# Narrow head-by-head loads and 64x64 attention tiles for nine of twenty-four chunks of a retention + MoE kernel

One core of one Trainium2 chip. The metric is the device time of one execution in microseconds, the slowest (here the only) core's; lower is better.

## The reference, cut to what matters

Linear attention with a decaying state for 4 batches, 8 heads, 768 tokens, head width 64; its output, 3072 tokens by 512, goes through a feed-forward block.

```python
for t in range(S):                        # attention, per batch and head
    state = gamma * state + outer(k[t], v[t])
    y[t] = scale * q[t] @ state
h = x @ w_in                              # x: 3072 x 512, w_in: 512 x 2048
s = np.sin(alpha * h)
out = (h + s * s / (alpha + 1e-09)) @ w_out
```

## The kernel before

The tokens are cut into 24 chunks of 128. Within a chunk attention is computed with masked scores; between chunks a 64x64 state per head is carried. Four first chunks of the batches come first, then the rest batch by batch. I call the index into `order` the *place* of a chunk, from 0: places 14 to 18 are chunks 1 to 5 of batch 2, places 19 to 23 those of batch 3.

```python
order = [b * NCH for b in range(B)]
order += [b * NCH + c for b in range(B) for c in range(1, NCH)]

def load_chunk(j, names="qkv"):           # 3 DMAs of 128 tokens x 8 heads x 64, float32 -> bfloat16
    ...
    nc.gpsimd.dma_start(out=t, in_=chunk_of(src, j))

def scale_v(j, eng):                      # v times its decay
    eng.tensor_mul(raw["v", j], raw["v", j], kg[:, j % NCH, :, None].to_broadcast([128, H, D]))

def turn(j):                              # q and k transposed by DMA, issued by SyncE
    nc.sync.dma_start_transpose(out=st["qkT", j], in_=raw["qk", j].rearrange("p i h d -> p (i h d)"))

def stage_A(j):                           # scores of a pair of heads: 64 rows x 128 columns
    for p in range(NP):
        for e in range(2):
            r = slice(64 * e, 64 * e + 64)
            nc.tensor.matmul(pa[:, e, p, :], qkT[r, NP + p, :], qkT[r, p, :], ...)
    nc.vector.tensor_mul(aT, pa, m)       # causal mask

def stage_M(j):                           # state times q, then v times scores; 128 rows x 64 columns
    ...
    nc.tensor.matmul(py[r, p, :], s_bd[c % 2][:, p, r], qkT[:, p, :], ...)
    ...
    nc.tensor.matmul(py[64 * e:64 * e + 64, p, :], vs[:, 2 * p + e, :], aT[:, e, p, :], ...)
    ps = stage_S(j) if c < NCH - 1 else None      # k times v into the state

# GpSimd's list: one in-order queue for loads and scalings
for n in range(11, NJ + 2):
    scale_v(P[n - 2], nc.gpsimd)
    if n < NJ:
        load_chunk(P[n])
    ...
```

The feed-forward block runs all the time: slots of four 512-column `ph` (w_in) and four `po` (w_out) multiplications. At fixed slots an attention burst is put between them: scores of place n, then output and state of place n-1.

## Time and profile before

| | before |
|---|---|
| time, median of the first 3 runs | 217.23 us (216.76 to 217.30) |
| span of the profiled run | 216.0 us |
| TensorE busy | 202.8 us, 94% |
| VectorE, ScalarE, GpSimd busy | 59%, 75%, 42% |
| GpSimd's loads (q0) | 13.37 MB, 88% of 16 engines' span |

"Busy" counts what an engine works on. q0 is the DMA queue of the loads that GpSimd issues; at 88% on average over the whole run it was full while it was used, for it is empty after 124 us. A *piece* of a load is the 64 numbers of one token of one head. The prediction shows the page's slices, the burst and GpSimd's list. A row of a timeline is: start and duration in us, engine, source line, operation, names, shapes, count, and in brackets the idle time before it and what ended it.

### The profile page before, as it was taken

The numbers are of one execution on the slowest core, as the hardware profiler recorded it, in microseconds if no ns is written. First come the engines' busy times: TensorE is split into PE (matmuls) and PEld (weight loads), VectorE is DVE, ScalarE is ACT, GpSimd is POOL, SyncE is SP. The second block draws the span as 40 slices with busy tenths as digits, with TensorE's granted clock in tenths as the row PEclk, the third lists the DMA queues.
The fourth block names the chain that finished last, engine by engine and source line by source line (L and its number), as shares of the span: only waits on it lengthen the run. The fifth ranks groups of instructions, "written<-read, shape, count | busy, mean of one in ns | idle before, by whom it ended". The sixth has DMA issues, their size and how long they took to land.

```text
span 216.0 us, 4277 instructions
## 1 busy us (share of the span) xinstructions
PE 202.8 (94%) x1658; PEld 108.5 (50%) x1685; DVE 127.9 (59%) x213; ACT 162.6 (75%) x311; POOL 90.0 (42%) x105
## 2 busy tenths in 40 slices
PE   7888898899989999999999999999999999999994
PEld 2444553457664555454554544554544544555554
DVE  5786759774896777765565565664644545333311
ACT  7778796468879988897787787787778877666630
POOL 8975332999395977786987200000000000000000
PEclk9999999999999999999999999999999999999999
DMA  9999999999999999999999942141011001111112
GB/s 130 154 189 189 206 207 167 143 116 214 185 138 194 123 151 173 131 177 146 174 146 144 126 100 71 26 102 50 2 49 52 15 33 49 52 49 49 52 49 97
DMA packets 100852, 24.93 MB, mean 115 GB/s; under 512 B 93392, under 2 KB 97888, under 8 KB 100832
## 3 DMA queue, kind: packets, MB, share of 16 engines
q0 software_dynamic: 77024, 13.37, 88.1%
q1 hardware_dynamic: 23808, 11.28, 26.3%
q8 instruction: 13, 0.21, 0.4%
q14 instruction: 7, 0.06, 0.1%
HBM read 27.27 MB, written 6.29 MB: 155 GB/s over the span
## 4 chain that ended last, share of the span: by engine, by line
PE 73%; DMA 13%; POOL 4%; DVE 4%; issue 2%; ACT 2%; POOLq 0%; DVEq 0%
PE po L304 32%; PE ph L279 30%; DMA qkr<-in_k_dram 8%; DMA w_in<-in_moe_w_in_dram 4%; PE py L247 3%; PE pa L213 2%; POOL qkr L83 2%; PE py L251 2%; PE poh L327 2%; DVE gT L294 2%; DVE aT L217 1%; POOL vr L83 1%; PE ps L227 1%; DVE xT L258 1%; ACT s L282 1%
## 5 line engine op out<-in xcount | busy, mean ns | idle before, releaser
L294 DVE SCALAR_TENSOR_TENSOR gT<-s,rec_alpha,ph 128x512 bf16<-128x512 f32 (+3 forms) x120 | 74.2, 638 | 71.5 <-ACT s L287 71.2
L279 PE MATMUL ph<-xT,w_in 128*128 128x512 bf16 (+3 forms) x477 | 97.7, 336 | 1.0 <-DMA w_in<-in_moe_w_in_dram 0.4
L282 ACT ACTIVATE s<-ph,alpha_sb 128x512 f32<-128x512 f32 (+3 forms) x120 | 69.6, 601 | 32.9 <-PE ph L279 32.4
L304 PE MATMUL po<-w_out,gT 128*128 128x512 bf16 x345 | 90.4, 379 | 3.3 <-issue 2.4
L279 PEld LDWEIGHTS <-w_in 128*128 128x128 bf16 x480 | 45.4, 98 | 42.1 <-issue 1.1
L287 ACT ACTIVATE s<-s 128x512 f32<-128x512 f32 (+1 forms) x94 | 58.4, 621 | 2.6
L304 PEld LDWEIGHTS <-gT 128*128 128x128 bf16 x368 | 33.9, 98 | 36.7 <-issue 0.6
L112 POOL TENSOR_TENSOR vr<-vr,kg 128x512 bf16<-128x512 bf16 x21 | 21.9, 1054 | 18.3 <-DMA vr<-in_v_dram 18.1
L217 DVE TENSOR_TENSOR aT<-pa,mask 128x1024 bf16<-128x1024 f32 x20 | 24.4, 1222 | 0.2 <-PE pa L213 0.2
L83 POOL DMA_DIRECT2D vr<-in_v_dram x24 | 21.8, 908 | 3.2 <-DMA w_in<-in_moe_w_in_dram 1.7
L83 POOL DMA_DIRECT2D qkr<-in_q_dram x23 | 21.3, 927 | 3.9 <-DMA w_out<-in_moe_w_out_dram 2.0
L83 POOL DMA_DIRECT2D qkr<-in_k_dram x23 | 20.5, 893 | 4.9 <-DMA w_out<-in_moe_w_out_dram 4.6
L234 ACT CAST s_bd<-ps 64x256 bf16<-64x256 f32 x40 | 14.4, 360 | 2.6 <-PE ps L227 2.1
L316 ACT COPY o_sb<-po 128x512 f32<-128x512 f32 x23 | 13.1, 576 | 3.9 <-PE po L304 3.7
L258 DVE TENSOR_TENSOR xT<-py,qg 128x512 bf16<-128x512 f32 x20 | 13.7, 684 | 1.3 <-PE py L251 1.3
L213 PE MATMUL pa<-qkT 64*128 64x128 bf16 x192 | 9.5, 219 | 1.2 <-DMA qkT<-qkr 0.6
L213 PEld LDWEIGHTS <-qkT 64*128 64x128 bf16 x192 | 5.4, 94 | 10.2 <-issue 6.7
L345 PE MATMUL spare<-warm 128*128 128x512 bf16 x27 | 9.0, 455 | 1.4 <-DVE warm L131 1.2
L251 PE MATMUL py<-aT,vr 128*64 128x128 bf16 x192 | 9.5, 220 | 0.4 <-DVE aT L217 0.4
L247 PE MATMUL py<-qkT,s_bd 128*64 128x128 bf16 x160 | 8.3, 225 | 0.0
L251 PEld LDWEIGHTS <-vr 128*64 128x64 bf16 x192 | 6.8, 110 | 1.3 <-issue 1.0
L247 PEld LDWEIGHTS <-s_bd 128*64 128x64 bf16 x160 | 5.1, 109 | 3.2 <-ACT s_bd L234 0.8
(61 smaller groups left out, 74.3 us busy)
## 6 DMA issues: line engine op xcount, KB each, us to landing
out_dram<-o_sb SPq DMA_DIRECT2D x23, 256.0 KB, 2.2
vr<-in_v_dram POOLq DMA_DIRECT2D x24, 128.0 KB, 6.3
qkr<-in_q_dram POOLq DMA_DIRECT2D x23, 128.0 KB, 5.6
qkr<-in_k_dram POOLq DMA_DIRECT2D x23, 128.0 KB, 5.9
w_in<-in_moe_w_in_dram POOLq DMA_DIRECT2D x4, 512.0 KB, 11.1
w_out<-in_moe_w_out_dram POOLq DMA_DIRECT2D x4, 512.0 KB, 15.0
qkT<-qkr SPq DMA_TRANSPOSE x17, 6.4
q<-in_q_dram SPq DMA_DIRECT2D x1, 256.0 KB, 3.3
```

Of the source, the lines that this page charges most:

```text
L83: nc.gpsimd.dma_start(out=t, in_=chunk_of(src, j))
L112: eng.tensor_mul(raw["v", j], raw["v", j], kg[:, j % NCH, :, None].to_broadcast([128, H, D]))
L213: nc.tensor.matmul(pa[:, e, p, :], qkT[r, NP + p, :], qkT[r, p, :], start=(p == 0), stop=True, skip_group_check=True)
L217: nc.vector.tensor_mul(aT.rearrange("p e n t -> p (e n) t"), pa.rearrange("p e n t -> p (e n) t"), m)
L247: nc.tensor.matmul(py[r, p, :], s_bd[c % 2][:, p, r], qkT[:, p, :], start=(p == 0), stop=True, skip_group_check=True)
L251: nc.tensor.matmul(py[64 * e:64 * e + 64, p, :], vs[:, 2 * p + e, :], aT[:, e, p, :], start=(c == 0 and p == 0), stop=True, skip_group_che ...
L258: nc.vector.tensor_mul(x, py, qg[:, c])
L279: nc.tensor.matmul(self.ph[:, m, :], w_in[:, i, f * 128:(f + 1) * 128], xT[g][:, i, self.lo:self.hi], start=(m == 0 and i == 0), stop=(i = ...
L282: nc.scalar.activation(out=self.s[:, m, :], in_=self.ph[:, m, :], func=ACTF.Sin, scale=alpha_sb[:, f:f + 1])
L287: nc.scalar.activation(out=self.s, in_=self.s, func=ACTF.Square)
L294: nc.vector.scalar_tensor_tensor(gT[self.g][:, f, self.lo:self.hi], self.s[:, m, :], rec_alpha[:, f:f + 1], self.ph[:, m, :], op0=ALU.mult ...
L304: nc.tensor.matmul(po[g, ts], gT[g][:, f, ts * C:(ts + 1) * C], w_out[:, f, :], start=(f == 0), stop=(f == FF - 1))
```

## The change

Nine chunks (places 15 to 18 and 19 to 23) become *wide*: heads 0 to 3 lie in partitions 0 to 63 and heads 4 to 7 in 64 to 127, tokens in halves of 64. Scores, mix and state then run in four 64x64 tiles of the array, and the masked quarter of the scores is skipped. Loads go head by head, for four or five chunks at once. The state is added up in SBUF by VectorE. In a wide burst, `inter` is state times q, `scores` is k times q of the next chunk, and `mix` is v times scores, followed by k times v into the state; `mix` needs the scaled v.

```diff
+    def load_seq(bt, names="qkv"):
+        ...
+            for h in range(H):
+                r = slice(64 * (h // NP), 64 * (h // NP) + 64)
+                o = tv[r, :, h % NP, :] if name == "v" else tqk[r, :, "qk".index(name), h % NP, :]
+                nc.gpsimd.dma_start(out=o, in_=src[bt, h, cs[0] * C:, :].rearrange("(f i) d -> i f d", i=64))
...
+    tiles4 = [(b, e) for b in range(2) for e in range(2)]
+    def scores(j):
+        for m in range(2):
+            for b, e in tiles4:
+                nc.tensor.matmul(pa[half(b), e, 192 * m:192 * m + 128]..., qkT[half(e), 2 + m, half(b)], ...)
+            for b, e in tiles4:
+                nc.tensor.matmul(pa[half(b), e, 192 * m + 128:192 * m + 192], qkT[half(e), 6 + m, half(b)], ...)
...
+    def burst(old, new, first=None):
+        inter(old)
+        return {**(scores(new) if new is not None else {}), **mix(old, first)}
...
-    for n in range(11, NJ + 2):
-        scale_v(P[n - 2], nc.gpsimd)
-        if n < NJ:
-            load_chunk(P[n])
-        ...
+    load_chunk(P[11])
+    scale_v(P[9], nc.gpsimd)
+    load_chunk(P[12])
+    scale_v(P[10], nc.gpsimd)
+    load_chunk(P[13])
+    scale_v(P[11], nc.gpsimd)
+    load_chunk(P[14])
+    scale_v(P[12], nc.gpsimd)
+    load_seq(2, "qk")
+    scale_v(P[13], nc.gpsimd)
+    scale_v(e2, nc.gpsimd)
+    scale_v(P[14], nc.gpsimd)
+    load_seq(2, "v")
+    scale_v(e3, nc.gpsimd)
+    load_seq(3, "qk")
+    for n in range(15, 19):
+        scale_v(P[n], nc.gpsimd)
+    load_seq(3, "v")
```

In the list the scaling of place 15 stands *behind* all q and k loads of batch 3.

More of the change, by code (lines that the diff above doesn't have):

```diff
@@ L77, in load_chunk @@
             if name == "v":
-                t = big.tile([128, H, D], BF16, name="vr", tag="vr", bufs=NJ)
+                t = big.tile([128, H, D], BF16, name="vr", tag="vr", bufs=NJ - 9)
             else:
                 if ("qk", j) not in raw:
-                    raw["qk", j] = big.tile([128, 2, H, D], BF16, name="qkr", tag="qkr", bufs=NJ)
+                    raw["qk", j] = big.tile([128, 2, H, D], BF16, name="qkr", tag="qkr", bufs=NJ - 10)
                 t = raw["qk", j][:, "qk".index(name)]
@@ L84, in load_chunk, with wide @@
             raw[name, j] = t
+    def wide(j):
+        return j >= 2 * NCH + 2 and j != 3 * NCH
+    def load_seq(bt, names="qkv"):
+        cs = [c for c in range(NCH) if wide(bt * NCH + c)]
+        nh = 2 * len(cs)
+        if "q" in names:
+            raw["seq", bt] = (big.tile([128, nh, 2, NP, D], BF16, name=f"qk_seq{bt}"),
+                              big.tile([128, nh, NP, D], BF16, name=f"v_seq{bt}"))
+        tqk, tv = raw["seq", bt]
+        for name, src in (("q", q), ("k", k), ("v", v)):
+            if name not in names:
+                continue
+            for h in range(H):
+                r = slice(64 * (h // NP), 64 * (h // NP) + 64)
+                o = tv[r, :, h % NP, :] if name == "v" else tqk[r, :, "qk".index(name), h % NP, :]
+                nc.gpsimd.dma_start(out=o, in_=src[bt, h, cs[0] * C:, :].rearrange("(f i) d -> i f d", i=64))
+        for i, c in enumerate(cs):
+            j, f = bt * NCH + c, slice(2 * i, 2 * i + 2)
+            raw["qk", j], raw["k", j], raw["v", j] = tqk[:, f], tqk[:, f, 1], tv[:, f]
     WP = 4
@@ L98 @@
     for name, src in (("q", q), ("k", k)):
-        near[name] = big.tile([128, H, D], F32, name=f"{name}0")
+        near[name] = work.tile([128, d_model], F32, name="o_sb", tag="o_sb", bufs=3).rearrange("i (h d) -> i h d", h=H)
         nc.sync.dma_start(out=near[name], in_=chunk_of(src, 0))
@@ L111, in scale_v @@
     def scale_v(j, eng):
-        eng.tensor_mul(raw["v", j], raw["v", j], kg[:, j % NCH, :, None].to_broadcast([128, H, D]))
+        t, by = raw["v", j], kg
+        if wide(j):
+            t, by = t.rearrange("i f p d -> i (f p) d"), kgq
+        eng.tensor_mul(t, t, by[:, j % NCH, :, None].to_broadcast([128, H, D]))
     load_chunk(0, "v")
@@ L157, with later_tables, later_mask @@
                          lg[:, None, :].to_broadcast([128, NCH, H]))
+    kgq = consts.tile([128, NCH, H], F32, name="kgq")
+    expoq = consts.tile([128, NCH, H], F32, name="expoq")
+    tok = consts.tile([128, NCH, 2], F32, name="tok")
+    lgq = consts.tile([128, NP], F32, name="lgq")
+    maskq = consts.tile([128, 192], BF16, name="maskq")
+    def later_tables():
+        for b in range(2):
+            r = slice(64 * b, 64 * b + 64)
+            for f in range(2):
+                nc.vector.tensor_scalar_add(tok[r, :, f], pos[r, :], float(64 * (f - b)))
+            nc.vector.tensor_copy(lgq[r], lg[r, NP * b:NP * b + NP])
+        for f in range(2):
+            nc.vector.tensor_mul(expoq[:, :, NP * f:NP * f + NP],
+                                 tok[:, :, f, None].to_broadcast([128, NCH, NP]),
+                                 lgq[:, None, :].to_broadcast([128, NCH, NP]))
+    def later_mask():
+        for b in range(2):
+            nc.vector.tensor_scalar(maskq[64 * b:64 * b + 64, 0:128], tio[64 * b:64 * b + 64],
+                                    tok[64 * b:64 * b + 64, 0, 0:1], None, op0=ALU.is_ge)
+        nc.vector.tensor_copy(maskq[:, 128:192], maskq[:, 0:64])
     qg = consts.tile([128, NCH, NP, C], F32, name="qg")
@@ L171 @@
     s_bd = [big.tile([128, NP, 128], BF16, name=f"s_bd{i}") for i in range(2)]
+    s_f = big.tile([128, NP, D], F32, name="s_f")
     st = {}
@@ L204, in turn @@
         st["qkT", j] = work.tile([128, 2 * NP, 128], BF16, name="qkT", tag="qkT", bufs=6)
-        nc.sync.dma_start_transpose(out=st["qkT", j], in_=raw["qk", j].rearrange("p i h d -> p (i h d)"))
+        nc.sync.dma_start_transpose(out=st["qkT", j], in_=raw["qk", j].rearrange(
+            "i a f p d -> i (a f p d)" if wide(j) else "i a h d -> i (a h d)"))
     def stage_A(j):
@@ L260, in stage_M, with half, inter @@
             keep_S(j, ps)
+    def half(x):
+        return slice(64 * x, 64 * x + 64)
+    tiles4 = [(b, e) for b in range(2) for e in range(2)]
+    def inter(j):
+        qkT, s = st["qkT", j], s_bd[j % NCH % 2]
+        st["py", j] = [psum.tile([128, 512], F32, name=f"py{b}", tag=tag) for b, tag in enumerate(("ps", "ty"))]
+        for m in range(2):
+            for b in range(2):
+                nc.tensor.matmul(st["py", j][b][:, m * 128:(m + 1) * 128].rearrange("p (f i) -> p f i", f=2),
+                                 s[:, 2 * b + m, :], qkT[:, m:m + 5:4, half(b)],
+                                 start=(m == 0), stop=True, skip_group_check=True)
@@ new lines, in scores @@
+    def scores(j):
+        qkT = st["qkT", j]
+        pa = psum.tile([128, 2, 512], F32, name="pa", tag="pa")
+        for m in range(2):
+            for b, e in tiles4:
+                nc.tensor.matmul(pa[half(b), e, 192 * m:192 * m + 128].rearrange("p (f i) -> p f i", f=2),
+                                 qkT[half(e), 2 + m, half(b)], qkT[half(e), m:m + 5:4, half(b)],
+                                 start=(m == 0), stop=True, skip_group_check=True)
+            for b, e in tiles4:
+                nc.tensor.matmul(pa[half(b), e, 192 * m + 128:192 * m + 192],
+                                 qkT[half(e), 6 + m, half(b)], qkT[half(e), 4 + m, half(b)],
+                                 start=False, stop=True, skip_group_check=True)
+        aT = work.tile([128, 2, 2, 192], BF16, name="aTw", tag="aT", bufs=2)
+        st["aT", j] = aT
+        return {"mask": lambda: nc.vector.tensor_mul(aT, pa[:, :, 0:384].rearrange("p e (m t) -> p e m t", m=2),
+                                                     maskq[:, None, None, :].to_broadcast([128, 2, 2, 192]))}
@@ new lines, in mix, with leave, keep, hand @@
+    def mix(j, first=None):
+        py, aT, vs, c = st["py", j], st["aT", j], raw["v", j], j % NCH
+        for m in range(2):
+            for b, e in tiles4:
+                nc.tensor.matmul(py[b][half(e), m * 128:(m + 1) * 128], vs[half(b), 0, 2 * m + e, :],
+                                 aT[half(b), e, m, 0:128], start=False, stop=True, skip_group_check=True)
+            for b, e in tiles4:
+                nc.tensor.matmul(py[b][half(e), m * 128 + 64:(m + 1) * 128], vs[half(b), 1, 2 * m + e, :],
+                                 aT[half(b), e, m, 128:192], start=False, stop=True, skip_group_check=True)
+        now = j if c < NCH - 1 else first
+        if now is not None:
+            ks, vs = raw["k", now], raw["v", now]
+            for f in range(2 if wide(now) else 1):
+                for m in range(2):
+                    for b, e in tiles4:
+                        h = 4 * b + 2 * m + e
+                        nc.tensor.matmul(py[b][half(e), 256 + 64 * m:320 + 64 * m],
+                                         ks[half(b), f, 2 * m + e, :] if wide(now) else ks[:, h, :],
+                                         vs[half(b), f, 2 * m + e, :] if wide(now) else vs[:, h, :],
+                                         start=False, stop=True, skip_group_check=True)
+        g, i = place[j]
+        if g not in xT:
+            xT[g] = work.tile([128, KS, sizes[g] * C], BF16, name="xT", tag="xT", bufs=3)
+        x = xT[g][:, :, i * C:(i + 1) * C]
+        def leave():
+            for b in range(2):
+                nc.vector.tensor_mul(x[:, 2 * b:2 * b + 2, :], py[b][:, 0:256].rearrange("p (m t) -> p m t", m=2),
+                                     qg[:, c, 2 * b:2 * b + 2])
+        def keep():
+            for b in range(2):
+                o, new = s_f[:, 2 * b:2 * b + 2], py[b][:, 256:384].rearrange("p (m d) -> p m d", m=2)
+                if wide(now):
+                    nc.vector.tensor_add(o, o, new)
+                else:
+                    nc.vector.tensor_copy(o, new)
+        def hand():
+            for e in range(2):
+                copy = nc.scalar.copy if now // NCH == 2 else nc.gpsimd.tensor_copy
+                copy(s_bd[(now % NCH + 1) % 2][half(e), :, half(e)], s_f[half(e)])
+        more = {"exit": leave}
+        if now is not None:
+            more.update(keep=keep, hand=hand)
+        return more
@@ L263, with run @@
+    def burst(old, new, first=None):
+        inter(old)
+        return {**(scores(new) if new is not None else {}), **mix(old, first)}
+    def run(more, *kinds):
+        for kind in kinds:
+            if more and kind in more:
+                more.pop(kind)()
     gT = {}
@@ L358 @@
     half_T(e0, 1, nc.scalar)
+    later_tables()
     nc.scalar.activation(out=kg, in_=expo, func=ACTF.Exp, scale=-1.0)
@@ L361 @@
         nc.scalar.activation(out=step[:, c, :], in_=lgp, func=ACTF.Exp, scale=float(C * c))
+    nc.scalar.activation(out=kgq, in_=expoq, func=ACTF.Exp, scale=-1.0)
     idle_work(2)
@@ L389 @@
     idle_work(3)
+    rest = [{}]
     def phase(g, outs, att, nf=1):
@@ L395, in phase @@
         for n in range(FF // nf):
+            more, fresh = rest[0], {}
             now = Slot(g, n * nf, nf=nf).sq("A")
+            run(more, "keep", "exit", "hand")
             for fn in att.get(n, ()):
-                fn()
+                fresh.update(fn() or {})
+            run(fresh, "mask")
+            if fresh:
+                rest[0] = fresh
             now.add()
@@ L464 @@
     b.add()
+    later_mask()
     a = Slot(0, 0, (n3, n4), 4)
@@ L511 @@
     scale_v(e1, nc.gpsimd)
-    for n in range(11, NJ + 2):
-        scale_v(P[n - 2], nc.gpsimd)
-        if n < NJ:
-            load_chunk(P[n])
-        if n in (13, 15):
-            scale_v(P[(n - 9) // 2], nc.gpsimd)
+    load_chunk(P[11])
[16 more added lines that the diff above has]
+    load_seq(3, "v")
     outs = out_pieces(0, (2, 3))
@@ L550, in at, with M_last, B @@
         atts[place[0]].setdefault(place[1], []).append(fn)
-    for n in range(10, NJ + 1):
-        if n < NJ:
-            at(where[n], A(P[n]))
-        if n > 10:
-            at(where[n], M(P[n - 1]))
-        if n < NJ and P[n] % NCH == 1:
-            at(where[n], SK(P[n] - 1))
+    def M_last(j):
+        stage_M(j)
+        nc.vector.tensor_copy(s_f, st["ps"])
+    def B(old, new, first):
+        return lambda: burst(old, new, first)
+    for n in range(10, NJ + 1):
+        new = P[n] if n < NJ else None
+        first = new - 1 if n < NJ and new % NCH == 1 else None
+        if n > 10 and wide(P[n - 1]):
+            at(where[n], B(P[n - 1], new, first))
+        else:
+            at(where[n], lambda j=new: (scores if wide(j) else stage_A)(j))
+            if n > 10:
+                at(where[n], lambda j=P[n - 1], last=wide(new): (M_last if last else stage_M)(j))
+            if first is not None:
+                at(where[n], SK(first))
         if n + 2 < NJ:
             at(where[n], X(P[n + 2]))
+        if n >= 19 and n < NJ:
+            at(where[n], lambda j=new: scale_v(j, nc.gpsimd))
     for g in range(2, NG):
```

## The prediction

> **What bounds the kernel now.** I read the page first (slices, then the chain that ended last), then the timeline of TensorE and of GpSimd around one attention burst, then the stretches and SyncE's waits.
>
> From the page, the slices and the chain by engine:
>
> ```profile
> PE   7888898899989999999999999999999999999994
> POOL 8975332999395977786987200000000000000000
> PEclk9999999999999999999999999999999999999999
> DMA  9999999999999999999999942141011001111112
> ...
> PE 73%; DMA 13%; POOL 4%; DVE 4%; issue 2%; ACT 2%; POOLq 0%; DVEq 0%
> ```
>
> One digit is 5.4 us. TensorE is full from about 65 us on, always at the full clock, and has 73% of the chain. But the DMA engines are full too until about 124 us, while GpSimd issues loads until 119 us: for half the run two resources are at their limit, and only one of them is named by the chain.
>
> The timeline of TensorE around one burst (start, duration, line):
>
> ```profile
> 102.85 1.03 PE L279 MATMUL ph<-xT,w_in 128*128 128x512 bf16 x4
> 103.81 0.40 PE L213 MATMUL pa<-qkT 64*128 64x128 bf16 x8
> 104.13 0.41 PE L247 MATMUL py<-qkT,s_bd 128*64 128x128 bf16 x8
> 104.38 0.39 PE L251 MATMUL py<-aT,vr 128*64 128x128 bf16 x8
> 104.60 0.29 PE L227 MATMUL ps<-vr,qkr 128*64 128x64 bf16 x8
> 105.05 0.81 PE L304 MATMUL po<-w_out,gT 128*128 128x512 bf16 x3 [0.16 <-issue]
> ```
>
> A 512-column multiplication takes 216 ns of the array (four start in 0.86 us), so ph ends its use at 102.85 + 0.86 = 103.71. Four po end at 105.70, where ph goes on (one po record is missing), so po began at 104.84. The burst costs 104.84 - 103.71 = **1.13 us**. Pairs of pa (and of both py) follow each other every 56 ns, pairs of ps every 30 ns: the 32 small multiplications are 4 x 56 + 4 x 56 + 4 x 56 + 4 x 30 = 0.79 us, and the rest is three changes of array shape of 0.09 to 0.11 us each.
>
> The timeline of GpSimd, early and in the same stretch; brackets say what ended a wait:
>
> ```profile
> 15.44 0.74 POOL L91 DMA_DIRECT2D w_in<-in_moe_w_in_dram  x1 [1.39 <-DMA w_in<-in_moe_w_in_dram]
> ...
> 101.43 1.04 POOL L112 TENSOR_TENSOR vr<-vr,kg 128x512 bf16<-128x512 bf16 x1 [1.87 <-DMA vr<-in_v_dram]
> 102.42 0.95 POOL L83 DMA_DIRECT2D qkr<-in_q_dram  x1
> 103.36 0.88 POOL L83 DMA_DIRECT2D qkr<-in_k_dram  x1
> 104.23 0.89 POOL L83 DMA_DIRECT2D vr<-in_v_dram  x1
> ...
> 109.23 1.04 POOL L112 TENSOR_TENSOR vr<-vr,kg 128x512 bf16<-128x512 bf16 x1 [0.43 <-DMA vr<-in_v_dram]
> ```
>
> I count chunks by their place in `order`, from 0. At 101.43 the v of place 18 has landed, at 109.23 that of place 20. Loads come only one to three places before they are used: SyncE's waits show its transposes waiting for loads nine times:
>
> ```profile
> SPq L205 <- DMA qkr<-in_k_dram: 24.4, 9, 6.2
> ```
>
> The row at 15.44 shows a second rule: the ninth load after w_in's first is not issued until that one has landed. At most 8 GpSimd loads are outstanding.
>
> **What the Trainium skill says.** "TensorEngine Tiling (Array Packing)", Tiling Modes, Key Properties: changing the mode drains the array, while tiles of one mode run in parallel. The trace agrees: 0.09 to 0.11 us at each change, and two half-array multiplications every 56 ns. "TensorE: Matmul & The Clock Gate", Part 3 (Packing small matmuls), lets row and column tiles be combined; no run yet shows four tiles. Its Part 1 says that an idle window of about 3.4 us halves the clock; this trace stays at 1.0 and has no such gap. "DMA: Bandwidth & Descriptors", Why a DMA increments its semaphore by 16 (How many engines), has a 128-partition transfer on 16 engines by divisibility; 64 also divides by 16, so I expect no loss from half the partitions. No run shows that yet.
>
> **The change part by part.**
>
> *Array time, on the path.* A wide burst has: inter, 4 full-array multiplications of 128 columns, 4 x 56 = 0.22, with no change of shape before it; one change, 0.09; scores, two rounds of four tiles at 128 columns (56 ns) and four at 64 (30 ns), plus 0.02 to start, 0.19; mix, the same without the start, 0.17; state, 16 of 64 columns in fours, 4 x 30 = 0.12; one change back, 0.11. Sum 0.92 instead of 1.13: **-0.2 us** from half of the masked triangle skipped and one change fewer. Nine such bursts; the last has no scores and the one that starts batch 3 has another change, so about eight gain: **-1.6 us** in all. Even with no overhead at all (0.64 streaming and two changes of 0.1, so 0.84) it would be -2.6 us. Two per cent is 4.3 us: the array cannot give it.
>
> *VectorE, beside.* The mask falls from 1.22 to about 0.94 us; two exits and two state additions replace one exit of 0.68. Some +0.2 us per burst on an engine 59% busy: free. ScalarE loses state copies of 0.73 us in batch 3: free.
>
> *Loads.* The bytes and the 256-byte pieces are the same, but 27 loads of 1024 pieces become 24 of 512 and 24 of 640, and their order changes. GpSimd issues a load of 1024 pieces in about 0.9 us and one of 512 (w_in, 128 x 4) in 0.74 to 0.8: I take 0.76 and 0.79, so 24.6 us of issue becomes 37 us. The order is what matters. Place 15 (the first wide chunk) is multiplied by its scaled v in the burst at 103.8, in the new order from 104.2. Its scaling stands in GpSimd's list behind the 16 q and k loads and the 8 v loads of batch 2 **and all 16 q and k loads of batch 3**.
> - By data: with 8 outstanding, the 16th of those cannot be issued before the 8th landed. By then 4 chunks (places 11 to 14) and all of batch 2's (8 x 3072 = 24,576 pieces) and 8 x 640 have landed: 29,696 pieces. The old kernel needed until just under 109.2 us for 30,720 pieces (places 11 to 20). With its engines full I give the deeper list at most 2 us: 106.5 to 108.5, plus 1.04 of scaling, about 107.5 to 109.5.
> - By issue: the v of place 12 lands near 70, so the list starts near 71.5; 16 x 0.76 ends near 84 to 86 (the later where data bounds it); three scalings 89; 8 x 0.76 gives 95; one scaling 96; 16 x 0.79 gives 109; scaling 110.
> So TensorE would go on at 108.5 to 110 instead of 104.2: **+4.3 to +5.8 us**, met once; later places are needed 8 us apart and gain slack. Smaller waits before it (all of batch 2's q and k, near 90, plus some 6 us for the transpose, against a use at 95.7) are contained in it, not added.
>
> *Tables.* Some ten small VectorE operations and one of ScalarE come near 7 us, a microsecond at most; TensorE waits for loads near 38 us anyway (2.5 us in all): hidden.
>
> Sum of the central case: 217.2 + 4.3 to 5.8 - 1.6 = 219.9 to 221.4.
>
> **The rivals.**
> 1. *No wait.* If the narrow loads land or issue faster than I think, only the array gain is left: 217.2 - 1.6 = 215.6. For it: the fifteenth chunk was deliberately left early, as by someone who watched these waits. Against it: DMA slices of 9 until 120 us, and the list order.
> 2. *The wait becomes worse.* If issue costs 0.9 whatever the pieces, 40 issues add some 5 us, to about 225; if TensorE idles over 3.4 us, the slow clock adds up to 1.7 us.
> 3. *TensorE cannot issue so fast.* The burst has 52 pairs of load and multiply instead of 32. The trace shows four instructions per 30 ns, not eight. At 30 ns per two tiles, scores, mix and state double to about 0.9 us, the burst becomes 1.35: +0.2 x 8 = 1.8 us instead of -1.6, so 219 without the wait.
> 4. *SyncE's queue stops behind a transpose that waits for batch 2's loads*, holding outputs back. Three output buffers, each used for 3 us or more, speak against more than a microsecond.
>
> **Range and chances.** Half weight to 220 to 221.5, three tenths to 215 to 217, two tenths to 222 to 226: centre 219.8 us, range 214.9 to 225.2. Faster by over 2% (under 212.9) needs what the array cannot give: 0.04. Slower by over 2% (over 221.6): 0.38. Within: 0.58.
>
> **What would show it.** Right: a single wait of TensorE of several us before the first wide mix, ended by GpSimd's scaling; that scaling starting at 107 or later, just after the last q and k load of batch 3; wide bursts near 0.92 us; no later waits. Wrong: scaling before 104; bursts over 1.13 us; loads of 512 pieces that cost GpSimd much less or more than 0.76 us; or a wait in a place that I called hidden (start, transposes of place 15, group boundaries where the exit now comes a slot later).

## The result, and the profile after

The changed kernel takes **226.06 us** (median of 4 runs, 224.01 to 226.55) against 217.26 (4 runs). The ratio is 1.038, interval 1.031 to 1.046: slower. (A ratio is the mean time of one kernel's fast runs over that of the other's from the same rounds, so not quite the ratio of the medians that are quoted.) The forecast had the direction (its centre was 219.8 us) but gave "slower by over 2%" only 0.38, and the time lies 0.9 us above the top of the range.

The page of the changed kernel, slices and chain by engine:

```profile
PE   7896898999979999999099999999999999999994
PEclk9999999999999999999769999999999999999999
DMA  9999999999999999999989713312111011111112
...
PE 49%; DMA 28%; POOL 20%; issue 1%; DVE 0%; POOLq 0%; DVEq 0%
```

A slice is 5.6 us here. TensorE has one empty slice (106 to 112 us), and in it and the next one the granted clock falls. The chain has moved: GpSimd and DMA now hold 48% of it, instead of 17%.

TensorE's waits in the changed kernel (total us, times, longest us):

```profile
PE py L354 <- POOL v_seq L137: 5.7, 1, 5.7
PE pa L265 <- DMA qkT<-qkr: 2.1, 2, 1.6
```

L354 is the first wide mix, L137 the scaling of v; L265 is stage_A. The timeline of TensorE around the first wide burst:

```profile
105.47 0.39 PE L327 MATMUL py<-qkT,s_bd 128*128 128x128 bf16 x4
105.79 0.25 PE L337 MATMUL pa<-qkT 64*64 64x128 bf16 x4
...
105.95 0.20 PE L341 MATMUL pa<-qkT 64*64 64x64 bf16 x4
111.85 0.32 PE L354 MATMUL py<-aTw,v_seq 64*64 64x128 bf16 x4 [5.70 <-POOL v_seq L137]
...
112.19 0.41 PE L366 MATMUL py<-v_seq,qk_seq 64*64 64x64 bf16 x16
112.53 1.89 PE L450 MATMUL po<-w_out,gT 128*128 128x512 bf16 x4
114.22 1.78 PE L425 MATMUL ph<-xT,w_in 128*128 128x512 bf16 x4
115.83 1.03 PE L450 MATMUL po<-w_out,gT 128*128 128x512 bf16 x4
```

The mix waits 5.70 us. Then four po take 114.22 - 112.53 = 1.69 us instead of 0.86, four ph 1.61: TensorE runs at half its clock. And GpSimd's list in the same stretch:

```profile
87.99 3.10 POOL L137 TENSOR_TENSOR vr<-vr,kg 128x512 bf16<-128x512 bf16 x3
90.99 5.50 POOL L103 DMA_DIRECT2D v_seq<-in_v_dram  x8
96.41 1.14 POOL L137 TENSOR_TENSOR vr<-vr,kg 128x512 bf16<-128x512 bf16 x1
97.40 5.09 POOL L103 DMA_DIRECT2D qk_seq<-in_q_dram  x7
104.30 0.72 POOL L103 DMA_DIRECT2D qk_seq<-in_q_dram  x1 [1.80 <-DMA v_seq<-in_v_dram]
105.00 5.73 POOL L103 DMA_DIRECT2D qk_seq<-in_k_dram  x8
110.64 4.14 POOL L137 TENSOR_TENSOR v_seq<-v_seq,kgq 128x512 bf16<-128x512 bf16 x4
```

The issue at 104.30 had waited for a v load of batch 2, the last of the eight, eight issues earlier. From then on v was there; but eight k loads of batch 3 came first, and the scaling began at 110.64.

The path from 216.0 to 224.0 us of span, read by comparing the start of the same multiplications in both traces:

| what has been passed | before, us | after, us | later by |
|---|---|---|---|
| last ph multiplication ahead of the scores of place 8 | 58.57 | 58.76 | 0.19 |
| the same, ahead of the scores of place 10 | 67.64 | 69.43 | 1.79 |
| the same, ahead of the first wide mix | 103.49 | 105.25 | 1.76 |
| first po after that burst | 104.84 | 112.53 | 7.69 |
| ahead of the next burst | 111.53 | 120.79 | 9.26 |
| ahead of the last burst | 181.57 | 189.57 | 8.00 |

So there are four terms: +1.6 between 58 and 68 us, +5.9 in the burst, +1.6 after it, and -1.3 from the later bursts.

### The profile page after: what moved, and what is told of

Its sections match the earlier page's. It is cut to its first block, busy times and chain, and to the rows that moved or that the text cites. A ratio compares the mean times of both kernels' runs of the same rounds, so it can differ in the third digit from the quotient of the medians.

```text
span 224.0 us, 4694 instructions
## 1 busy us (share of the span) xinstructions
PE 206.9 (92%) x1849; PEld 109.8 (49%) x1849; DVE 131.2 (59%) x250; ACT 159.9 (71%) x302; POOL 103.5 (46%) x136
## 4 chain that ended last, share of the span: by engine, by line
PE 49%; DMA 28%; POOL 20%; issue 1%; DVE 0%; POOLq 0%; DVEq 0%
PE po L450 25%; PE ph L425 19%; DMA vr<-in_v_dram 8%; DMA w_out<-in_moe_w_out_dram 8%; POOL qk_seq L103 5%; POOL qkr L83 5%; DMA qk_seq<-in_q_dram 5%; DMA w_in<-in_moe_w_in_dram 4%; POOL vr L137 4%; DMA v_seq<-in_v_dram 4%; POOL vr L83 2%; POOL v_seq L103 2%; PE poh L473 2%; PE py L327 1%; PE pa L337 1%
## 5 line engine op out<-in xcount | busy, mean ns | idle before, releaser
L83 POOL DMA_DIRECT2D vr<-in_v_dram x15 | 13.7, 911 | 3.5 <-DMA w_in<-in_moe_w_in_dram 1.7
L83 POOL DMA_DIRECT2D qkr<-in_q_dram x14 | 12.8, 918 | 4.7 <-DMA w_in<-in_moe_w_in_dram 1.6
L103 POOL DMA_DIRECT2D qk_seq<-in_q_dram x16 | 11.3, 737 | 6.9 <-DMA qkr<-in_q_dram 2.8
L269 DVE TENSOR_TENSOR aT<-pa,mask 128x1024 bf16<-128x1024 f32 x11 | 13.4, 1218 | 1.6 <-PE pa L265 1.6
L83 POOL DMA_DIRECT2D qkr<-in_k_dram x14 | 12.5, 893 | 3.3 <-DMA w_out<-in_moe_w_out_dram 3.3
L137 POOL TENSOR_TENSOR vr<-vr,kg 128x512 bf16<-128x512 bf16 x12 | 12.7, 1076 | 3.0 <-DMA vr<-in_v_dram 3.0
L137 POOL TENSOR_TENSOR v_seq<-v_seq,kgq 128x512 bf16<-128x512 bf16 x9 | 9.3, 1087 | 7.1 <-DMA v_seq<-in_v_dram 6.8
L103 POOL DMA_DIRECT2D qk_seq<-in_k_dram x16 | 11.2, 735 | 0.7 <-DMA qk_seq<-in_q_dram 0.5
L103 POOL DMA_DIRECT2D v_seq<-in_v_dram x16 | 11.3, 760 | 0.0
L346 DVE TENSOR_TENSOR aTw<-pa,maskq 128x768 bf16<-128x768 f32 x9 | 8.6, 954 | 0.7
```

The source lines that it names most:

```text
L103: nc.gpsimd.dma_start(out=o, in_=src[bt, h, cs[0] * C:, :].rearrange("(f i) d -> i f d", i=64))
L137: eng.tensor_mul(t, t, by[:, j % NCH, :, None].to_broadcast([128, H, D]))
L269: nc.vector.tensor_mul(aT.rearrange("p e n t -> p (e n) t"), pa.rearrange("p e n t -> p (e n) t"), m)
```

## The experiments

Ratios are against the kernel before, run on the same chip in the same rounds (one slow run of the kernel before, 219.89 us, is left out).

| run | time, us (median) | ratio (95%) |
|---|---|---|
| changed kernel | 226.06 | 1.038 (1.031 to 1.046) |
| e1_scale_early | 217.80 | 1.000 (0.992 to 1.008) |
| e2_before_ahead | 218.47 | 1.007 (0.999 to 1.014) |
| e3_after_old_order | 222.05 | 1.021 (1.014 to 1.029) |
| e4_both | 216.50 | 0.996 (0.988 to 1.004) |
| e5_batch3_only | 216.49 | 0.997 (0.994 to 1.000) |
| e4_again | 215.95 | 0.994 (0.990 to 0.997) |
| e6_keep_warm | 223.57 | 1.030 (1.026 to 1.035) |

### e1_scale_early: is it the order of the list?

```diff
-    load_seq(3, "qk")
-    for n in range(15, 19):
+    load_seq(3, "q")
+    scale_v(P[15], nc.gpsimd)
+    load_seq(3, "k")
+    for n in range(16, 19):
```

> The changed kernel, with the scaling of the first wide chunk (place 15) put between the eight q loads and the eight k loads of batch 3 instead of behind all sixteen. List-order theory: v of batch 2 has landed by about 104.3 us (an issue that waited for it went on then), so the scaling starts near 105 instead of 110.6, the wait of TensorE before the first wide mix falls from 5.7 us to under 0.5, the slow clock after it (1.6 us) goes too, and the time falls by about 7 us to 218.5 to 219.5. Landing theory (the narrow v loads themselves are late, or scaling is slow): the scaling still starts after 109 and the time stays above 224.

Measured: 217.80 us, so about 8 us less by moving one instruction. GpSimd's timeline in this run:

```profile
97.24 5.95 POOL L103 DMA_DIRECT2D qk_seq<-in_q_dram  x8
103.16 1.09 POOL L137 TENSOR_TENSOR v_seq<-v_seq,kgq 128x512 bf16<-128x512 bf16 x1
104.88 5.75 POOL L103 DMA_DIRECT2D qk_seq<-in_k_dram  x8 [0.63 <-DMA qk_seq<-in_q_dram]
110.56 3.12 POOL L137 TENSOR_TENSOR v_seq<-v_seq,kgq 128x512 bf16<-128x512 bf16 x3
```

The scaling of place 15 began at 103.16, and TensorE's list of waits no longer has the mix. The other three still began at 110.56, and nothing waited for them. The landing theory falls: v was there at 103.16, 7.5 us before the time at which the changed kernel scaled it. The order of the list is shown as the cause of the long wait.

This run holds a second finding. Its early wait was much as in the changed kernel, and a slow clock followed it there too:

```profile
62.50 0.40 PE L265 MATMUL pa<-qkT 64*128 64x128 bf16 x8 [1.90 <-DMA qkT<-qkr]
...
64.39 1.92 PE L425 MATMUL ph<-xT,w_in 128*128 128x256 bf16 x8
```

Eight ph of 256 columns took 1.92 us where they take 1.04 at full clock. So e1's profiled run had paid for the collision of the next experiment, and for 3.4 us of half clock, and still came out level with the kernel before.

### e2_before_ahead: do loads issued sooner collide with the transposes?

```diff
     for n in range(11, NJ + 2):
+        if n < 15:
+            load_chunk(P[n])
         scale_v(P[n - 2], nc.gpsimd)
-        if n < NJ:
+        if 15 <= n < NJ:
             load_chunk(P[n])
```

> The kernel before with one thing from the change: the loads of places 11 to 14 are issued ahead of the scaling of places 9 to 12 instead of behind it. Collision theory (loads issued some 4 us sooner share the DMA engines with the transposes of places 8 to 10): the transposes of places 8 to 10 take about 9 to 10 us instead of 7 to 8, TensorE waits for them some 2 us instead of 0.6 around 58 to 64 us, and the time rises by 1 to 1.7 us to about 218.5. Rival (that wait of the changed kernel came from its later start): the same time as the kernel before, within 0.3 us.

Measured: 218.47 us, ratio 1.007; the interval just includes 1. TensorE's wait is as long as was expected. The kernel before:

```profile
61.82 0.40 PE L213 MATMUL pa<-qkT 64*128 64x128 bf16 x8 [0.55 <-DMA qkT<-qkr]
```

and this run:

```profile
62.57 0.40 PE L213 MATMUL pa<-qkT 64*128 64x128 bf16 x8 [2.41 <-DMA qkT<-qkr]
```

Both wait for the transpose of place 9. The starts show that only 0.75 us of the longer wait is a later landing; for the other 1.1 us TensorE merely came to it sooner in this run (at 60.16 instead of 61.27 us), so the length of the wait overstates the cost. What the earlier loads do is seen in the transposes themselves, in all nine traces: that of place 9 takes 8.0 to 9.0 us from issue to landing in the four with the earlier loads (changed, e1, e2, e6) and 6.5 to 6.8 in the five without; that of place 10 takes 9.7 to 10.2 us with them and 6.5 to 7.3 without. Those of places 11 and 12 rose from 4.8 and 7.1 us in the kernel before to 9.6 and 9.9 here. That of place 8 hardly changed (8.3 and 8.6 us). The longer transposes are shown to come with the earlier loads; the total, by its interval, only makes 1 us likely.

### e3_after_old_order: the collision taken out of the changed kernel

```diff
-    load_chunk(P[11])
-    scale_v(P[9], nc.gpsimd)
-    ... (and so on to)
-    load_chunk(P[14])
-    scale_v(P[12], nc.gpsimd)
+    for n in range(11, 15):
+        scale_v(P[n - 2], nc.gpsimd)
+        load_chunk(P[n])
```

> The changed kernel with the loads of places 11 to 14 put back behind the scaling of places 9 to 12, nothing else. Collision theory: the wait of TensorE near 60 us falls from 2.1 to about 0.6. What the total does tells whether waits add: if the end of GpSimd's list fixes an absolute time for the first wide mix, the wait there only grows by what was saved and the total stays at 225 to 227; if the waits are independent, it falls by 1.6 us to about 224.4.

Measured: 222.05 us, 4 us less. Neither expectation had that. The wait for the transposes is gone, as expected, but the long wait shrank as well:

```profile
PE py L354 <- POOL v_seq L137: 3.5, 1, 3.5
```

and GpSimd's timeline says why:

```profile
72.62 4.81 POOL L103 DMA_DIRECT2D qk_seq<-in_q_dram  x7
...
78.26 5.46 POOL L103 DMA_DIRECT2D qk_seq<-in_k_dram  x8
83.63 3.15 POOL L137 TENSOR_TENSOR vr<-vr,kg 128x512 bf16<-128x512 bf16 x3
...
105.57 4.10 POOL L137 TENSOR_TENSOR v_seq<-v_seq,kgq 128x512 bf16<-128x512 bf16 x4
```

The list that was issued *later* at its beginning ended 110.64 - 105.57 = 5.1 us *earlier*. Batch 2's q and k took GpSimd from 72.6 to 83.6 without a pause to speak of; in the changed kernel they took from 71.3 to 88.0, with waits of 2.76, 1.03 and 0.76 us for loads eight issues back. Counted in the trace, 19,289 pieces of loads were started between 60 and 90 us in the changed kernel and 20,886 here. So issuing sooner made the loads arrive later. The 5.1 us are those of one pair of traces; the other runs have the same sign. The last v load of batch 2 landed at 104.0, 101.6 and 101.6 us with the early order (changed, e1, e6) and at 97.0, 100.0 and 98.2 with the old one (e3, e4_both, e4_again), about 4 us sooner, and the pieces started between 60 and 90 us were 19,289 to 19,424 against 20,565 to 21,034. The clearest difference in the traces is that in the changed kernel the transposes of places 10 to 13 take 9.4 to 10.2 us each, so that two are in flight most of the time, and in e3 5.4 to 6.8, overlapping less. Whether that overlap is what costs the engines time was not tried and stays open.

### e4_both and e4_again: both edits

The diffs of e1 and e3 together.

> Both edits: early scaling of place 15 and the old order of places 11 to 14. If the whole account is right (1.6 us collision, 5.7 us wait, 1.6 us slow clock, minus 1.7 us of shorter bursts and 0.2 us of start), the time is 217.26 + 0.2 - 1.5 = about 216, unless loads that now start later make place 15 late again: then a wait of up to 2 us is left and the time is 217 to 218. Rival: there is a cost I have not named, and it stays above 219.

Measured: 216.50 us, ratio 0.996, 0.988 to 1.004, near the sum of the account. One of four runs (218.15 us, clock 0.99) looked like another wait. (In the profiled run the scaling of place 15 ended at 102.10 and the mix began at 103.10 us: 1 us to spare.)

> The same kernel as e4_both once more, in five rounds, for a narrower interval: e4_both had a ratio of 0.996 with an interval of 0.988 to 1.004. By the ledger (eight bursts at 0.21 us less, 0.2 us more at the start) it should be 0.993 to 0.995. If the runs of 217 to 218 us (one at a clock of 0.99) come back in half of the runs, the wait for the first wide chunk sits on an edge and the mean stays near 0.997.

Measured: 215.95 us, ratio 0.994, 0.990 to 0.997: **faster than the kernel before by 0.6%, and faster than the changed kernel by some 10 us.** The interval excludes 1. No run was over 216.5 us, and in the profiled one the scaling ended at 101.02, 2.7 us ahead of the mix. The ratio lies in the expected 0.993 to 0.995; the interval leaves room for an unnamed cost or gain of 0.7 us.

### e5_batch3_only: the same without the tight part

Only batch 3 is wide (`wide(j)` becomes `j > 3 * NCH`; loads to place 18 as before; the narrow loads stand at the end).

> Only the five chunks of batch 3 are wide; places 4 to 18 are loaded and computed as in the kernel before, in its order, and the narrow loads of batch 3 come at the end of the list, where nothing needs them for 10 us. If the account is right, no new wait of TensorE appears and four bursts of 0.92 instead of 1.13 us are left as gain: 0.8 to 1 us, less 0.2 us for the tables, so a ratio of 0.996 to 0.998. If narrow loads slow the whole load stream by themselves, the waits near 60 us stay as before (they come earlier) but transposes of places 16 to 19 get late and the time rises by over 1 us.

Measured: 216.49 us, ratio 0.997, 0.994 to 1.000, as expected, though the interval reaches 1. TensorE has no new wait. The gain agrees with the number of wide bursts, as far as intervals of 0.3% can tell, and comes without a wait on an edge.

### e6_keep_warm: is the slow stretch the clock?

```diff
+        more = scores(new) if new is not None else {}
+        if old == P[15]:
+            keep_warm = psum.tile([128, 512], F32, name="keep_warm", tag="mm", bufs=4)
+            for _ in range(22):
+                nc.tensor.matmul(keep_warm, warm[:, :128], warm, start=True, stop=True)
-        return {**(scores(new) if new is not None else {}), **mix(old, first)}
+        return {**more, **mix(old, first)}
```

> The changed kernel with 22 multiplications of 512 columns on a constant tile (4.75 us of array time, result unused) between the scores and the first wide mix, inside the wait of 5.7 us. Clock theory: the wait is filled, the granted clock stays at 1.0, the four po and four ph after it take 0.86 instead of 1.69 and 1.61 us, and the time falls by about 1.6 us from 226.1 to 224.5. Rival (the slow multiplications after the wait come from something else, as late operands): they stay slow and the time does not fall.

Measured: 223.57 us, 2.5 less than the changed kernel (226.06; the two ratios, each against its own rounds, differ by 0.8%, 1.7 us). The granted clock was 1.0 throughout the profiled run. TensorE's timeline in this run:

```profile
104.49 4.92 PE L405 MATMUL keep_warm<-warm 128*128 128x512 bf16 x21
110.72 0.25 PE L354 MATMUL py<-aTw,v_seq 64*64 64x128 bf16 x4 [1.32 <-POOL v_seq L137]
...
110.92 0.30 PE L366 MATMUL py<-v_seq,qk_seq 64*64 64x64 bf16 x16
...
112.02 1.03 PE L430 MATMUL ph<-xT,w_in 128*128 128x512 bf16 x4
112.89 1.03 PE L455 MATMUL po<-w_out,gT 128*128 128x512 bf16 x4
```

The ph after the wait take 0.87 us again, the sixteen state multiplications 0.30 instead of 0.41. The clock is shown as the cause of the slow stretch. The profiled spans differ by 3.0 us (224.0 and 221.0): 1.8 is the clock, and 1.1 that the mix went on sooner (110.72 instead of 111.85), because the scaling began at 109.61 here. That second part has nothing to do with the clock, so the total alone would not have decided. Useless work made the kernel faster.

## Why the prediction was wrong, point by point

- **The long wait was predicted and came**: one wait of TensorE, before the first wide mix, ended by GpSimd's scaling, which stood behind batch 3's k loads. e1 shows that the order alone made it.
- **Its size was the step that failed**: "So TensorE would go on at 108.5 to 110 instead of 104.2: +4.3 to +5.8 us". It went on at 111.85, 7.65 us later. Two terms below that step were wrong, in opposite senses. "I take 0.76 and 0.79" for an issue was too much: 5.50 / 8 = 0.69 and 5.73 / 8 = 0.72 us, 3 us less over 40 issues. And the same sum left at most 2 us for waits for outstanding loads ("84 to 86"): between 71 and 111 us GpSimd stood 7.6 us between such issues, 6.8 of it shown as waits for loads eight issues back, and the first sixteen ended at 88.0. "With its engines full I give the deeper list at most 2 us" had the wrong sign: the eighth q load of batch 3, foreseen for 106.5 to 108.5, landed at 109.57, later than the 109.16 at which the old kernel had its 30,720 pieces; in e3, with the shallower list, it landed at 103.06.
- **Why it had the wrong sign**: I treated the load queue as full and so indifferent to what is issued when. With the earlier loads the transposes, which run on the same 16 engines, became 9 to 10 us long and the load stream itself slower. How the one makes the other stays open (see e3). I had written that a wait "in a place that I called hidden" would show me wrong; one came at 58 to 64 us, in a place I had not named, the transposes of places 8 and 9. e2 shows that wait with the earlier loads alone, e3 its absence without them. It is contained in the 7.65 us, not added, as the prediction said of smaller waits.
- **The slow clock stood only in a rival** ("adds up to 1.7 us"). It came, 1.57 us in the two groups after the burst and about 0.26 in the burst itself; e6 shows it. A wait of over 4 us that I myself predicted should have carried its own price in the central sum.
- **The array's gain was right.** Wide bursts take 0.92 us (121.93 - 121.01), predicted 0.92; narrow ones 1.13. The terms of the prediction add up to 0.91, so the last digit of the match is luck. The four tiles run in parallel, and TensorE has no trouble issuing 52 pairs, so rival 3 falls. The gain is 1.28 us after the first wide burst (six times 0.2, and 0.08 for the one that starts batch 3) and 0.2 in the first one, after its wait: 1.5 instead of 1.6.
- **The tables were hidden** as said: 1.06 us later near 20 us, where TensorE waited for a load of k, but only 0.19 from 39 us on.
- **No later waits**, as said.
- **One line was misread by one**: the row at 15.44 is the eighth load after w_in's first, the ninth with that one counted. "At most 8 outstanding" stands.

Summed: 7.65 + 0.26 + 1.57 - 0.2 (the first burst's own gain) - 1.28 = 8.0 us, the difference of the spans. The rival that came nearest was the second, by its clock half.

## What to carry to other kernels

An in-order engine that both issues transfers and computes has a deadline for each computation; put the computation at the first place in the list where its data is there, not behind the transfers of a later stage: one line moved was worth 8 us here. Loading further ahead was not free where the same engines also carry transfers that something waits for: the deeper list made both the transposes and its own end later. When a wait of TensorE of several us is foreseen, add the slow clock after it to its cost (1.8 us after 5.7 us here).

## What the Trainium skill lacked or had wrong

- "TensorE: Matmul & The Clock Gate", Part 1: the half clock is there as described, and its stretches are multiples of the page's window (6.8 us in the changed kernel, 3.4 us in e1_scale_early). But its rule of no idle gaps over some 3.4 us is too lenient: in e1 a wait of 1.9 us was followed by the half clock, while a wait of 2.4 us in e2_before_ahead's profiled run was not. The page's free-running window explains this in the nine traces. Within a trace the changes of the clock lie whole multiples of 3.41 us apart; cut at these times, every window at full clock with 1.90 us or more of idle TensorE was followed by the half clock (1.90 in e1, 2.04 in e3, 2.30 at the end of e5, 2.75 in the changed kernel), and none with 1.76 or less was. In e2 a boundary cuts the wait in two, and its window with most idle time has 1.76. Where the limit lies between 1.76 and 1.90 us is not shown.
- The same page, Part 1, says that starts never come closer than about 25 ns. That holds per tile. With four tiles, sixteen multiplications of 64 columns, each about 0.19 us long, took 0.30 us in e6: (0.30 - 0.19) / 15 = 7 ns from start to start. Its Part 3, on packing, agrees that tiles start closer together.
- "TensorEngine Tiling (Array Packing)" gives no cost for a change of mode; here 0.09 to 0.11 us each, and three became two.
- "DMA: Bandwidth & Descriptors", DMA Transpose (X-bar), does not tell what a transpose costs beside a stream of loads: a transpose of 128 x 1024 bf16 landed 3.0 to 3.1 us after its issue alone, 4 to 8 us beside the loads of the kernel before, and 9 to 10 us with loads always queued.
- I found no page with the time that one issue takes GpSimd by the number of its pieces: 0.69 us for 512 pieces of 64 elements, 0.72 for 640, 0.9 for 1024.
